# Expert slots: token numbers loaded two slots ahead, results stored by ScalarE's queue, a clamp on VectorE

## The chip, the core and the metric

The kernel runs on one core of a Trainium2 chip. The core has TensorE (PE, with its weight loads shown apart as PEld), VectorE (DVE), ScalarE (ACT), GpSimd (POOL) and SyncE (SP), which issues most of the transfers. The metric is the device time of one execution in microseconds; the time before is the median of three runs, 1485.05 us (1483.12 to 1486.98).

## The reference, cut to what matters

A linear attention makes a matrix x of 4608 tokens by 512. A router gives every token one of eight experts; each expert is a two-layer network with 512 x 1024 and 1024 x 512 weights. A last two-layer network (512 x 2048 x 512) follows.

```python
logits = x @ w_gate + modality_bias[modality_id]
e_idx = np.argmax(logits, axis=1)
gate_w = softmax(logits)[np.arange(N), e_idx]
for e in range(8):
    mask = e_idx == e
    out[mask] = gate_w[mask, None] * (np.maximum(x[mask] @ w1[e], 0.0) @ w2[e])
h = out @ w_in
out = np.maximum(0.01 * h, h) @ w_out
```

## The kernel before

The program has four stages, one after the other: attention and routing (to about 198 us of the span), the experts (to 720 us), the first half of the last network (the class Hidden, to about 1110 us) and its second half. The order of the instructions on every engine is the order in which the code is written; the attention alone is sorted by a table of times.

**Routing.** At its end `phase_r` computes for every token a row number in the DRAM table `region`, in which each expert's tokens lie together, and POOL scatters pairs (token number, gate weight) into it from the tile `tg` (line 384, one indirect DMA for 128 tokens). `tg` has two buffers; ScalarE writes the token numbers into it (line 326). `phase_r` runs five times, the last two for six and three groups of 128 tokens.

**Slots.** The experts' work is cut into slots of 512 tokens of one expert. The table `ti`, computed on the chip, holds for each slot the expert, the place in `region` and the place in the result. SP reads these numbers into registers with `reg` (line 505: a load of one number, then register work) before it issues a transfer with such an address. Ten slots, 0 to 9, are executed here: nine of them unconditional, the others behind a test of their number.

**Inside a slot.** `slot(s)` (line 648) first calls `xload(s + 1)`: SP loads the next slot's 512 pairs from `region` into one of two tiles `idt`, VectorE casts the token numbers to integers (`idi`, line 543), and POOL gathers the rows of x with four indirect DMAs (`xg`, line 545). Then come eight `pass1(f)`, each of 12 matmuls into a bank `hp` of three; ScalarE writes `hh` from it (line 566) and VectorE `hl` (line 567), and a bank is free once its `hl` is written. ScalarE scales `xg` by the gate weights (`xgate`, line 551). Then come four `pass2(s, t)` of 24 matmuls into `yp`; ScalarE copies `yp` into one of two tiles `y` (line 581), and SP stores `y` into the DRAM matrix `dense` (line 582). In the second and third of them TensorE transposes the next slot's `xg` (line 556). Floating numbers are multiplied as a high and a low part; `split` (line 474) makes the high part on ScalarE (line 475) and the low part on VectorE (line 476). Between the passes, `wsplit` splits the weights, which SP loads into a ring of six tiles `st` (line 517).

**The conversions.** The last network's weights come as 64-bit numbers. `f64` (line 597) turns one block of 128 x 1024 such numbers into 32-bit parts, in steps that the slots call: `step()` stands after `pass1(f)` for odd f and after each `pass2`, so two blocks are converted in each of the slots 0 to 7. A block's steps are: the mask on VectorE (610) and the clamp on POOL (611), then two shifts on VectorE (615 and 616; 616 works on the clamped numbers), then two bit operations (618, 619), then four sums (623) and a split into `rh` and `rl`. The first step also has SP store the block before (627, 628) and load the next one (`w`, 594).

SP issues in order. In a slot its queue holds weight loads that wait for a free tile of the ring, the loads and stores of the conversions, the load of `idt`, and the stores of `y`:

```python
nc.sync.dma_start(out=idt.rearrange("p t c -> p (t c)"), in_=region[bass.ds(r, SLOT), :]...)
nc.vector.tensor_copy(out=idi, in_=idt[:, :, 0])
...
nc.scalar.copy(out=y, in_=yp)
nc.sync.dma_start(out=dense[128 * d:128 * d + 128, bass.ds(o, SLOT)], in_=y)
```

Before slot 8 the kernel also has SP load the first tokens of `dense` for the next stage (`xr`, line 755).

Of the kernel before, what the change touches and what calls it, by code (L numbers as in the profile page):

```python
# [9 lines left out]
F32 = mybir.dt.float32  # L10
# [3 lines left out]
AF = mybir.ActivationFunctionType  # L14
ALU = mybir.AluOpType
# [78 lines left out]
def attention(ctx, tc, cst, a, region, xd):  # L94

    nc = tc.nc
    ident, onesf, trib, onesb, biasT, tokid = cst["id"], cst["one"], cst["trib"], cst["oneb"], cst["biasT"], cst["tok"]
    kp = ctx.enter_context(tc.tile_pool(name="kp", bufs=2))
    sp = ctx.enter_context(tc.tile_pool(name="sp", bufs=2))
# [8 lines left out]
    for i in range(4):  # L108
        t = one.tile([128, 4, 146], F32, name=f"kvx{i}")
# [193 lines left out]
    def phase_r(i, c0, c1):  # L303
# [3 lines left out]
        t, rp = {}, {}  # L307

        def r0():
            lr, ri = st_b[i]  # L310
            t["lp"] = sp.tile([128, NC, 8, NE], F32, tag="lp", name="lp", bufs=1)[:, 0:n]
            for x in ("lg", "ex", "w"):
                t[x] = sp.tile([128, NC, NE], F32, tag=x, name=x)[:, 0:n]
            for x in ("mx", "gs"):
                t[x] = sp.tile([128, NC], F32, tag=x, name=x)[:, 0:n]
            for x in ("oh", "st"):
                t[x + "f"] = sp.tile([128, 80], F32, tag=x, name=x)[:, 0:NE * (n + 1)]
                t[x] = t[x + "f"].rearrange("p (e c) -> p e c", e=NE)
            t["tot"] = sp.tile([128, NE], F32, tag="tot", name="tot")
            t["tb"] = sp.tile([128, 2, NE], BF16, tag="tb", name="tb")  # L320
            t["ix"] = sp.tile([128, NC], I32, tag="ix", name="ix")
            t["tg"] = sp.tile([128, NC, 2], F32, tag="tg", name="tg")
            nc.vector.tensor_tensor(out=t["lp"].rearrange("p c (q j) e -> p (c q) j e", q=4),
                                    in0=lr[:, cs].rearrange("p c q (j e) -> p (c q) j e", j=2),
                                    in1=bc(ri[:, cs].rearrange("p c q j -> p (c q) j"), 3, NE), op=ALU.mult)
            nc.scalar.copy(out=t["tg"][:, 0:n, 0], in_=tokid[:, NC * i + c0:NC * i + c1])
# [96 lines left out]
TIMES = {'kmax0': 0.52, 'kmax_t0': 2.07, 'kmax_m0': 2.08, 'kmax_b0': 2.81, 'kexp00': 5.69, 'kexp01': 5.14, 'kmax1': 2.61, 'kmax_t1': 3.96, 'kmax_m1': 3.97, 'kmax_b1': 4.96, 'kexp10': 10.5, 'kexp11': 10.37, 'kv00': -0.98, 'kv01': 1.26, 'kvn00': 1.27, 'kv02': 2.34, 'kv03': 3.62, 'kvn01': 3.63, 'kvT0': 4.15, 'kg0': 5.58, 'kv10': 4.78, 'kv11': 5.01, 'kvn10': 6.83, 'kv12': 7.04, 'kv13': 7.05, 'kvn11': 7.18, 'kvT1': 9.53, 'kg1': 10.5, 'qmax0': 3.34, 'qsub0': 4.01, 'qmax1': 4.06, 'qsub1': 4.45, 'qmax2': 5.72, 'qsub2': 7.63, 'load_k': 7.3, 'load_v': 7.4, 'load_q': 9.28, 'r0': -0.92, 'r1': -0.1, 'r2': 1.0, 'r3': 1.01, 'r4': 1.02, 'r5': 1.03, 'r6': 1.04, 'r7': 1.25, 'r8': 2.6, 'r9': 2.78, 'r10': 3.29, 'r11': 3.3, 'r12': 3.31, 'r13': 3.32, 'r14': 3.33, 'r15': 3.34, 'r16': 3.61, 'scat0': 5.13, 'scat1': 4.64, 'scat2': 7.54, 'scat3': 7.51, 'scat4': 7.24, 'scat5': 8.2, 'scat6': 7.81, 'scat7': 5.6, 'scat8': 9.07, 'trans0': -1.5, 'trans1': -0.08, 'trans2': 0.44, 'trans3': 0.93, 'trans4': 2.62, 'trans5': 2.55, 'trans6': 4.49, 'trans7': 4.66, 'trans8': 6.15, 'xmm0': 0.52, 'xmm1': 0.81, 'xmm2': 1.45, 'xmm3': 3.52, 'xmm4': 4.14, 'xmm5': 5.5, 'xmm6': 6.45, 'xmm7': 7.52, 'xmm8': 10.5, 'evac0': 0.56, 'evac1': 1.32, 'evac2': 3.1, 'evac3': 4.3, 'evac4': 4.91, 'evac5': 5.51, 'evac6': 7.1, 'evac7': 8.89, 'evac8': 10.51, 'prep': -0.05, 'rar0': 5.7, 'rbr0': 0.2, 'rar1': 5.78, 'rbr1': 0.3, 'rar2': 5.86, 'rbr2': 0.4, 'rar3': 5.94, 'rbr3': 0.5, 'rar4': 6.02, 'rbr4': 0.6, 'rar5': 6.1, 'rbr5': 0.7, 'rar6': 6.18, 'rbr6': 0.8, 'rar7': 6.26, 'rbr7': 0.9, 'rar8': 6.34, 'rbr8': 1.0, 'rar9': 6.42, 'rbr9': 1.1, 'rar10': 6.5, 'rbr10': 1.2, 'rar11': 6.58, 'rbr11': 1.3, 'rar12': 6.66, 'rbr12': 1.4, 'rar13': 6.74, 'rbr13': 1.5, 'rar14': 6.82, 'rbr14': 1.6, 'rar15': 6.9, 'rbr15': 1.7, 'rar16': 6.98, 'rbr16': 1.8, 'rascat0': 7.3, 'rascat1': 7.31, 'rascat2': 7.32, 'rascat3': 7.33, 'rascat4': 7.34, 'rascat5': 7.35, 'rbscat0': 2.0, 'rbscat1': 2.01, 'rbscat2': 2.02}  # L423


SP = mybir.EngineType.SP
CLAMP_LO = float(np.array(0x38000000, np.int32).view(np.float32))
CLAMP_HI = float(np.array(0x47EFFFFF, np.int32).view(np.float32))

# [49 lines left out]
def experts(ctx, tc, cst, a, region, xd, dense, did, wops, pre):  # L479
# [14 lines left out]
    hl = wp.tile([128, 8, SLOT], F32R, name="hl")  # L494
    ring = [wp.tile([128, 1024], F32, name=f"st{i}") for i in range(6)]
    NST = len(ring)
    idts = [wp.tile([128, 4, 2], F32, name=f"idt{i}") for i in range(2)]
    idis = [wp.tile([128, 4], I32, name=f"idi{i}") for i in range(2)]
    xg = wp.tile([128, 4, DM], F32, name="xg")
    ys = [wp.tile([128, DM], F32, name=f"y{i}") for i in range(2)]  # L500
# [1 line left out]
    stage, regs = {}, {}  # L502

    def reg(s, f, mx):
        return nc.values_load(ti[0:1, 3 * s + f:3 * s + f + 1], engines=[SP], min_val=0, max_val=mx)

    def wload(s, which, c):
        t = stage[s, which, c] = ring[cnt[0] % NST]
# [14 lines left out]
    def loads_to(n):  # L523
        while nload[0] < min(n, len(items)):
            wload(*items[nload[0]])
            nload[0] += 1

    def wsplit(s, which, c):
# [6 lines left out]
            split(nc, w2h[:, 2 * c:2 * c + 2], w2l[:, 2 * c:2 * c + 2], t.rearrange("p (k f) -> p k f", k=2))  # L535
        loads_to(n + 1 + AHEAD)

    def xload(s):
        r = reg(s, 1, NE * NT)
        idt, idi = idts[s % 2], idis[s % 2]  # L540
        nc.sync.dma_start(out=idt.rearrange("p t c -> p (t c)"),
                          in_=region[bass.ds(r, SLOT), :].rearrange("(p t) c -> p (t c)", t=4))
        nc.vector.tensor_copy(out=idi, in_=idt[:, :, 0])
        for t in range(4):
            nc.gpsimd.indirect_dma_start(out=xg[:, t], out_offset=None, in_=xd,  # L545
                                         in_offset=bass.IndirectOffsetOnAxis(ap=idi[:, t:t + 1], axis=0),
                                         bounds_check=NT - 1, oob_is_err=False)

    def xgate(s):
        for t in range(4):  # L550
            nc.scalar.activation(out=xg[:, t], in_=xg[:, t], func=AF.Copy, scale=idts[s % 2][:, t, 1:2])

    def xprep(k):
        tp = ps2.tile([128, 4, 128], F32, tag="tp", name="tp")
# [15 lines left out]
    def pass2(s, d, o, mid):  # L570
        yp = ps.tile([128, SLOT], F32, tag="y", name="yp")
        n = 0
        for f in range(8):
            for w, h in ((w2h, hh), (w2l, hh), (w2h, hl)):
                nc.tensor.matmul(yp, lhsT=w[:, f, 128 * d:128 * d + 128], rhs=h[:, f], start=(n == 0), stop=(n == 23))  # L575
                n += 1
            if f == 3:
                mid()
        y = ys[cnt[1] % 2]
        cnt[1] += 1  # L580
        nc.scalar.copy(out=y, in_=yp)
# [15 lines left out]
    def f64(cv, name, i, w, ahead, behind):  # L597

        V = nc.vector
        if name == "win":  # L600
            dst = wops["win"][i % 4].rearrange("p s h k f -> h k p s f")[:, i // 4]
        else:
            dst = wops["wout"].rearrange("s p h k f -> h k p s f")[:, i]
        w2 = w.rearrange("p b f w -> p (b f) w")
        lo, hi = w2[:, :, 0], w2[:, :, 1]
        r = cv.tile([128, 8, 256], F32, tag="r", name="r")
        rh = cv.tile([128, 7, 256], F32R, tag="rh", name="rh")
        rl = cv.tile([128, 7, 256], F32R, tag="rl", name="rl")
        t = r[:, 0:4].rearrange("p b f -> p (b f)").bitcast(I32)
        V.tensor_scalar(out=t, in0=hi, scalar1=0x7FFFFFFF, scalar2=None, op0=ALU.bitwise_and)  # L610
        nc.gpsimd.tensor_scalar(out=t.bitcast(F32), in0=t.bitcast(F32), scalar1=CLAMP_LO, scalar2=CLAMP_HI, op0=ALU.max, op1=ALU.min)
        behind()
        ahead()
        yield
        V.tensor_scalar(out=lo, in0=lo, scalar1=29, scalar2=0x40000000, op0=ALU.logical_shift_right, op1=ALU.bitwise_xor)
        V.tensor_scalar(out=t, in0=t, scalar1=4, scalar2=1, op0=ALU.logical_shift_left, op1=ALU.logical_shift_right)
        yield
        V.tensor_tensor(out=t, in0=t, in1=lo, op=ALU.bitwise_xor)
        V.scalar_tensor_tensor(out=t, in0=hi, scalar=-0x80000000, in1=t, op0=ALU.bitwise_and, op1=ALU.bitwise_or)
        yield  # L620
# [27 lines left out]
    def slot(s, step=lambda: None, mid2=lambda t: None):  # L648
# [442 lines left out]
```

## Time and profile before

| | |
|---|---|
| time, median of three runs | 1485.05 us |
| profiled execution: its time, its span | 1477.94 us, 1476.2 us |
| PE busy | 1338.4 us, 91% of the span |
| PEld busy | 1229.8 us, 83% |
| DVE busy | 1031.6 us, 70% |
| ACT busy | 600.5 us, 41% |
| POOL busy | 403.9 us, 27% |
| mean granted clock of TensorE | 0.968 of full speed |

The profile shows one execution. "Busy" is the time in which an engine executes; register work and the issue of transfers are not counted. An idle time stands in brackets before the instruction that ended it, with what released it. A row of SPq is a transfer's issue by SP, not its flight; from issue to landing is told apart. The granted clock is given as a share of 2.4 GHz.

### The profile page before, as it was taken

What the parts mean: (1) busy time and instruction counts of PE and PEld (TensorE: products, weight loads), DVE (VectorE), ACT (ScalarE), POOL (GpSimd) and SP (SyncE); (2) the same over time, 40 slices, a digit from 0 to 9 for tenths busy, and PEclk for the clock granted to TensorE, in tenths of its full rate; (3) what the DMA queues carried; (4) which work ended last, traced back from release to release, by engine and by line L of the source; (5) the groups of instructions that cost most, each with busy time, mean ns of one, the idle gap of its engine ahead of it and who ended that gap; (6) DMA issues with size and microseconds to landing.
All of it is one profiled execution on the core that took longest, in us unless ns stands there. A gap on an engine that the chain in (4) does not pass through costs nothing.

```text
span 1476.2 us, 23214 instructions
## 1 busy us (share of the span) xinstructions
PE 1338.4 (91%) x9083; PEld 1229.8 (83%) x9083; DVE 1031.6 (70%) x1347; ACT 600.5 (41%) x946; POOL 403.9 (27%) x273
## 2 busy tenths in 40 slices
PE   4778718999999999989989999999989999999998
PEld 3668606777777777768889999999989999999998
DVE  5788626677767767634558777777767777777775
ACT  3566414555455545534423223332324333333332
POOL 2447532313231323011033434333331111101111
PEclk9899958999999999989999999999999999999999
DMA  9564245877787779565583333333297443443430
GB/s 374 205 241 154 103 133 171 260 242 233 249 274 232 232 246 305 194 221 179 184 346 144 121 137 136 122 133 125 103 417 295 143 143 117 135 133 118 143 115 30
DMA packets 144519, 280.05 MB, mean 190 GB/s; under 512 B 17808, under 2 KB 69520, under 8 KB 141456
## 3 DMA queue, kind: packets, MB, share of 16 engines
q1 hardware_dynamic: 125376, 218.94, 44.0%
q10 hardware_dynamic: 11472, 38.52, 6.4%
q0 software_dynamic: 7552, 21.02, 4.0%
q8 instruction: 74, 1.21, 0.3%
q14 instruction: 45, 0.37, 0.1%
HBM read 181.59 MB, written 96.85 MB: 189 GB/s over the span
## 4 chain that ended last, share of the span: by engine, by line
issue 26%; DVE 9%; PE 6%; POOL 6%; DMA 2%; ACT 1%; POOLq 0%; SPq 0%; DVEq 0%
PE hp L778 6%; POOL out L959 3%; POOL s L818 2%; DMA wi<-wid 2%; DVE ht L791 1%; DVE ht L824 1%; DVE ht L827 1%; DVE s L815 1%; DVE ht L811 1%; DVE s L813 1%; DVE x L476 1%; POOL s L819 1%; DVE xl L476 0%; ACT ht L820 0%; ACT xh L475 0%
## 5 line engine op out<-in xcount | busy, mean ns | idle before, releaser
L778 PE MATMUL hp<-xh,wi 128*128 128x256 f32 x1152 | 212.9, 281 | 3.7 <-DVE ht L827 2.3
L937 PE MATMUL yp<-wi,x 128*128 128x256 f32 x1152 | 191.5, 284 | 0.0
L778 PEld LDWEIGHTS hp<-xh,wi 128*128 128x128 f32 x1152 | 179.4, 188 | 6.3 <-DVE ht L827 3.8
L937 PE MATMUL yp<-wi,wi 128*128 128x256 f32 x1200 | 178.3, 283 | 0.3 <-DVE wi L476 0.3
L778 PE MATMUL hp<-x,wi 128*128 128x256 f32 x1296 | 166.7, 289 | 8.1 <-DMA wi<-wid 3.9
L778 PEld LDWEIGHTS hp<-x,wi 128*128 128x128 f32 x1296 | 163.1, 197 | 8.9 <-DVE ht L827 4.1
L937 PEld LDWEIGHTS yp<-wi,wi 128*128 128x128 f32 x1200 | 163.5, 192 | 0.5 <-DVE wi L476 0.5
L937 PEld LDWEIGHTS yp<-wi,x 128*128 128x128 f32 x1152 | 161.9, 192 | 0.1
L778 PE MATMUL hp<-xl,wi 128*128 128x256 f32 x576 | 160.8, 279 | 0.0
L564 PE MATMUL hp<-xh,w1h 128*128 128x512 f32 x320 | 129.7, 405 | 27.8 <-DVE hl L567 27.8
L959 POOL DMA_INDIRECT out<-yo,idx x36 | 47.4, 1317 | 314.9 <-DVE idx L953 294.3
L564 PE MATMUL hp<-xl,w1h 128*128 128x512 f32 x320 | 127.6, 399 | 0.0
L564 PE MATMUL hp<-xh,w1l 128*128 128x512 f32 x320 | 127.2, 397 | 0.0
L575 PE MATMUL yp<-hh,w2h 128*128 128x512 f32 x320 | 126.4, 395 | 0.0
L575 PE MATMUL yp<-hl,w2h 128*128 128x512 f32 x320 | 124.8, 390 | 0.0
L575 PE MATMUL yp<-hh,w2l 128*128 128x512 f32 x320 | 124.7, 390 | 0.0
L545 POOL DMA_INDIRECT xg<-xd,idi x44 | 58.3, 1325 | 237.5 <-DVE hl L567 216.8
L818 POOL TENSOR_TENSOR s<-s,s 128x512 f32<-128x512 f32 x36 | 48.3, 1343 | 226.4 <-DVE s L815 160.8
L778 PEld LDWEIGHTS hp<-xl,wi 128*128 128x128 f32 x576 | 108.0, 187 | 0.0
L791 DVE SCALAR_TENSOR_TENSOR ht<-ht 128x1024 f32<-128x1024 f32 x72 | 104.8, 1455 | 2.5
L476 DVE TENSOR_TENSOR w1l<-st,w1h 128x1024 fp32r<-128x1024 f32 x44 | 53.8, 1227 | 71.3 <-ACT w1h L475 71.3
L564 PEld LDWEIGHTS hp<-xh,w1h 128*128 128x128 f32 x320 | 61.9, 193 | 46.9 <-DVE hl L567 34.1
(202 smaller groups left out, 2629.4 us busy)
## 6 DMA issues: line engine op xcount, KB each, us to landing
st<-in_w SPq DMA_DIRECT2D x89, 512.0 KB, 5.1
hd<-ht ACTq DMA_DIRECT2D x72, 512.0 KB, 3.2
xt<-hd SPq DMA_DIRECT2D x18, 1024.0 KB, 5.4
hr<-hd SPq DMA_DIRECT2D x18, 1024.0 KB, 5.5
wi<-wid SPq DMA_DIRECT2D x28, 512.0 KB, 8.4
wi<-wod SPq DMA_DIRECT2D x6, 2048.0 KB, 13.2
v<-in_v SPq DMA_DIRECT2D x8, 1300.0 KB, 13.0
dense<-y SPq DMA_DIRECT2D x40, 256.0 KB, 3.3
```

Of the source, the lines that this page charges most:

```text
L476: nc.vector.tensor_tensor(out=lo, in0=src, in1=hi.bitcast(F32), op=ALU.subtract)
L545: nc.gpsimd.indirect_dma_start(out=xg[:, t], out_offset=None, in_=xd, in_offset=bass.IndirectOffsetOnAxis(ap=idi[:, t:t + 1], axis=0), bou ...
L564: nc.tensor.matmul(hp, lhsT=w[:, k, 128 * f:128 * f + 128], rhs=x[:, k], start=(n == 0), stop=(n == 11))
L575: nc.tensor.matmul(yp, lhsT=w[:, f, 128 * d:128 * d + 128], rhs=h[:, f], start=(n == 0), stop=(n == 23))
L778: self.nc.tensor.matmul(bank[:, g], lhsT=w[:, h, k, 128 * g:128 * g + 128], rhs=x[:, k], start=(n == 0), stop=(n == 5))
L791: V.scalar_tensor_tensor(out=c, in0=c, scalar=0.01, in1=c, op0=ALU.mult, op1=ALU.max)
L811: V.tensor_tensor(out=h[:, 0, 0], in0=bank, in1=s[1], op=ALU.add)
L813: V.tensor_tensor(out=s[6], in0=bank, in1=s[1], op=ALU.add)
L815: V.tensor_tensor(out=s[7], in0=bank, in1=s[6], op=ALU.add)
L818: G.tensor_tensor(out=s[6], in0=s[6], in1=s[5], op=ALU.add)
L937: nc.tensor.matmul(bank, lhsT=x[:, k], rhs=w[i][:, h, k], start=(c == 0), stop=(c == 23))
L959: ins = nc.gpsimd.indirect_dma_start(out=out, out_offset=bass.IndirectOffsetOnAxis(ap=idi[s % 2][:, t:t + 1], axis=0), in_=y[:, t], in_off ...
```

## The change

Five edits, all but the first in the experts' stage.

The tile `tg` gets a third buffer. The load of a slot's pairs becomes a function of its own, `idload`, with three tiles `idt` in place of two. It is called for slots 0 and 1 before the stage's first weights (for slot 0 as the very first transfer, then two weight loads, then slot 1), and in slot s for slot s + 2, behind the copy of slot s's pairs into `did`. The store of `y` is issued by ScalarE, for which `reg` loads the place in the result into a register of ScalarE too. The clamp of the conversions is computed by VectorE, right behind the mask.

```diff
-            t["tg"] = sp.tile([128, NC, 2], F32, tag="tg", name="tg")
+            t["tg"] = sp.tile([128, NC, 2], F32, tag="tg", name="tg", bufs=3)
...
-    idts = [wp.tile([128, 4, 2], F32, name=f"idt{i}") for i in range(2)]
+    idts = [wp.tile([128, 4, 2], F32, name=f"idt{i}") for i in range(3)]
...
-        return nc.values_load(ti[0:1, 3 * s + f:3 * s + f + 1], engines=[SP], min_val=0, max_val=mx)
+        return nc.values_load(ti[0:1, 3 * s + f:3 * s + f + 1], engines=[SP] + [ACT] * (f == 2), min_val=0, max_val=mx)
...
+    def idload(s):
+        if s < NSLOT:
+            nc.sync.dma_start(out=idts[s % 3].rearrange("p t c -> p (t c)"),
+                              in_=region[bass.ds(reg(s, 1, NE * NT), SLOT), :].rearrange("(p t) c -> p (t c)", t=4))
+
     def xload(s):
-        r = reg(s, 1, NE * NT)
-        idt, idi = idts[s % 2], idis[s % 2]
-        nc.sync.dma_start(out=idt.rearrange("p t c -> p (t c)"),
-                          in_=region[bass.ds(r, SLOT), :].rearrange("(p t) c -> p (t c)", t=4))
+        idt, idi = idts[s % 3], idis[s % 2]
         nc.vector.tensor_copy(out=idi, in_=idt[:, :, 0])
...
         nc.scalar.copy(out=y, in_=yp)
-        nc.sync.dma_start(out=dense[128 * d:128 * d + 128, bass.ds(o, SLOT)], in_=y)
+        nc.scalar.dma_start(out=dense[128 * d:128 * d + 128, bass.ds(o, SLOT)], in_=y)
...
         V.tensor_scalar(out=t, in0=hi, scalar1=0x7FFFFFFF, scalar2=None, op0=ALU.bitwise_and)
-        nc.gpsimd.tensor_scalar(out=t.bitcast(F32), in0=t.bitcast(F32), scalar1=CLAMP_LO, scalar2=CLAMP_HI, op0=ALU.max, op1=ALU.min)
+        V.tensor_scalar(out=t.bitcast(F32), in0=t.bitcast(F32), scalar1=CLAMP_LO, scalar2=CLAMP_HI, op0=ALU.max, op1=ALU.min)
...
         nc.sync.dma_start(out=did[bass.ds(o, SLOT)].rearrange("(p t) c -> p (t c)", t=4),
-                          in_=idts[s % 2].rearrange("p t c -> p (t c)"))
+                          in_=idts[s % 3].rearrange("p t c -> p (t c)"))
+        idload(s + 2)
...
+    idload(0)
+    loads_to(2)
+    idload(1)
     loads_to(AHEAD)
     xload(0)
     wsplit(0, 1, 0)
```

SP's queue at the start of the experts' stage before the change; `st_1856` to `st_1861` are the ring's six tiles, `idt_1862` slot 0's pairs, and TENSOR_LOAD reads a number into a register:

```order
L517 DMA st_1856<-in_w 128x4x256
...
L517 DMA st_1860<-in_w 128x2x512
L505 TENSOR_LOAD ti
L505 ISA x2
L541 ISA
L541 DMA idt_1862<-region 128x8
L517 ISA
L517 DMA st_1861<-in_w 128x2x512
```

And the same place after it:

```order
L540 DMA idt_1862<-region 128x8
L505 TENSOR_LOAD ti
L505 ISA x2
L517 ISA
L517 DMA st_1856<-in_w 128x4x256
...
L517 DMA st_1857<-in_w 128x4x256
...
L540 DMA idt_1863<-region 128x8
...
L517 DMA st_1858<-in_w 128x4x256
```

Slot 0's pairs moved from behind five weight loads to the front of them, and slot 1's pairs, which were loaded at the start of slot 0, stand three transfers behind.

ScalarE's queue at the end of slot 0 before the change, from the third `pass2` on; `y_1867` and `y_1868` are the two result tiles, and `rh` and `hh` are as in the text above:

```order
L581 COPY y_1867<-yp 128x512
L475 CAST w1h<-st_1860 128x4x256
L581 COPY y_1868<-yp 128x512
L475 CAST w1h<-st_1861 128x4x256
L475 CAST rh<-r 128x1792
L566 ACTIVATE hh<-hp 128x512
```

And after it:

```order
L583 COPY y_1868<-yp 128x512
L584 ISA
L584 DMA dense<-y_1868 128x512
L475 CAST w1h<-st_1860 128x4x256
L583 COPY y_1869<-yp 128x512
...
L584 DMA dense<-y_1869 128x512
L475 CAST w1h<-st_1861 128x4x256
L475 CAST rh<-r 128x1792
```

Between each copy of a result and the cast of the next weights now stands the store, which has to wait for the copy.

## Rows read from the trace of the kernel before

**Rows 1.** Waits of 185 to 740 us: engine, line, releaser: total us, times, longest

```profile
DVE r L616 <- POOL r L611: 32.6, 9, 4.6
DVE idi L543 <- DMA idt<-region: 32.3, 4, 11.6
ACT y L581 <- DMA dense<-y: 28.5, 6, 5.6
...
PE hp L564 <- DVE hl L567: 27.8, 15, 9.7
...
PE tp L556 <- ACT xg L551: 25.9, 10, 22.6
...
ACT tg L326 <- DMA region<-tg,ix: 7.1, 1, 7.1
```

**Rows 2.** Two slots as stretches: us; busy (instructions) by engine; clock, DMA share, GB/s

```profile
383.40:433.00 49.60, 47.26 (x208) 38.77 (x208) 35.88 (x42) 24.04 (x31) 12.61 (x6) 0.97 0.77 245
...
529.50:577.50 48.00, 46.41 (x209) 37.58 (x209) 34.52 (x42) 24.32 (x31) 12.68 (x6) 1.00 0.78 254
```

**Rows 3.** Timeline of the stage's start: start us, us, engine, line [idle before <-releaser]

```profile
196.41 0.97 POOL L384 DMA_INDIRECT region<-tg,ix  x1 [0.30 <-issue]
196.67 2.92 SPq L517 DMA_DIRECT2D st<-in_w  x5
...
201.82 0.35 SPq L541 DMA_DIRECT2D idt<-region  x1
...
207.28 0.17 DVE L543 CAST idi<-idt 128x4 int32<-128x4 f32 x1 [11.64 <-DMA idt<-region]
...
213.81 0.47 PE L556 MATMUL tp<-cf,xg 128*128 128x128 f32 x1 [22.57 <-ACT xg L551]
```

**Rows 4.** Timeline of slot 0, its first pass

```profile
226.75 1.02 SPq L594 DMA_DIRECT2D w<-in_win  x2
...
236.00 0.17 DVE L543 CAST idi<-idt 128x4 int32<-128x4 f32 x1 [8.65 <-DMA idt<-region]
...
236.83 0.79 PE L564 MATMUL hp<-xh,w1h 128*128 128x512 f32 x1 [5.92 <-DVE hl L567]
...
240.84 0.41 PE L564 MATMUL hp<-xh,w1h 128*128 128x512 f32 x1
```

**Rows 5.** Timeline of slot 8, its first pass

```profile
633.53 0.17 DVE L543 CAST idi<-idt 128x4 int32<-128x4 f32 x1 [8.89 <-DMA idt<-region]
...
634.35 0.79 PE L564 MATMUL hp<-xh,w1h 128*128 128x512 f32 x1 [9.68 <-DVE hl L567]
...
640.06 0.46 PE L564 MATMUL hp<-xl,w1h 128*128 128x512 f32 x1
```

**Rows 6.** Timeline of two slot ends, with the next slots' first waits

```profile
424.32 0.59 ACT L581 COPY y<-yp 128x512 f32<-128x512 f32 x1 [5.59 <-DMA dense<-y]
...
433.09 0.50 PE L564 MATMUL hp<-xh,w1h 128*128 128x512 f32 x1 [2.38 <-DVE hl L567]
...
444.66 0.50 PE L564 MATMUL hp<-xh,w1h 128*128 128x512 f32 x1 [0.38 <-DVE hl L567]
...
520.72 0.59 ACT L581 COPY y<-yp 128x512 f32<-128x512 f32 x1 [3.91 <-PE yp L575]
...
529.50 0.50 PE L564 MATMUL hp<-xh,w1h 128*128 128x512 f32 x1 [0.70 <-DVE hl L567]
```

**Rows 7.** Instructions of lines 616 and 788: ns min/median/max, first and last start

```profile
L616 DVE TENSOR_SCALAR r<-r x16: 671/694/697, 246.9 to 608.7; 128x1024 int32<-128x1024 int32 x16
...
L788 ACTq DMA_DIRECT2D hd<-ht x72: 326/326/335, 737.4 to 1111.3; - x72
```

**Rows 8.** Issue to landing of lines 582 (dense), 541 (idt), 594 (w)

```profile
DMA to landing us min/median/max: 2.0/3.3/10.0
...
DMA to landing us min/median/max: 3.0/3.5/7.4
...
DMA to landing us min/median/max: 7.0/10.1/12.0
```

More of the change, by code (lines that the diff above doesn't have):

```diff
@@ L423 @@
 TIMES = {'kmax0': 0.52, 'kmax_t0': 2.07, 'kmax_m0': 2.08, 'kmax_b0': 2.81, 'kexp00': 5.69, 'kexp01': 5.14, 'kmax1': 2.61, 'kmax_t1': 3.96, 'kmax_m1': 3.97, 'kmax_b1': 4.96, 'kexp10': 10.5, 'kexp11': 10.37, 'kv00': -0.98, 'kv01': 1.26, 'kvn00': 1.27, 'kv02': 2.34, 'kv03': 3.62, 'kvn01': 3.63, 'kvT0': 4.15, 'kg0': 5.58, 'kv10': 4.78, 'kv11': 5.01, 'kvn10': 6.83, 'kv12': 7.04, 'kv13': 7.05, 'kvn11': 7.18, 'kvT1': 9.53, 'kg1': 10.5, 'qmax0': 3.34, 'qsub0': 4.01, 'qmax1': 4.06, 'qsub1': 4.45, 'qmax2': 5.72, 'qsub2': 7.63, 'load_k': 7.3, 'load_v': 7.4, 'load_q': 9.28, 'r0': -0.92, 'r1': -0.1, 'r2': 1.0, 'r3': 1.01, 'r4': 1.02, 'r5': 1.03, 'r6': 1.04, 'r7': 1.25, 'r8': 2.6, 'r9': 2.78, 'r10': 3.29, 'r11': 3.3, 'r12': 3.31, 'r13': 3.32, 'r14': 3.33, 'r15': 3.34, 'r16': 3.61, 'scat0': 5.13, 'scat1': 4.64, 'scat2': 7.54, 'scat3': 7.51, 'scat4': 7.24, 'scat5': 8.2, 'scat6': 7.81, 'scat7': 5.6, 'scat8': 9.07, 'trans0': -1.5, 'trans1': -0.08, 'trans2': 0.44, 'trans3': 0.93, 'trans4': 2.62, 'trans5': 2.55, 'trans6': 4.49, 'trans7': 4.66, 'trans8': 6.15, 'xmm0': 0.52, 'xmm1': 0.81, 'xmm2': 1.45, 'xmm3': 3.52, 'xmm4': 4.14, 'xmm5': 5.5, 'xmm6': 6.45, 'xmm7': 7.52, 'xmm8': 10.5, 'evac0': 0.56, 'evac1': 1.32, 'evac2': 3.1, 'evac3': 4.3, 'evac4': 4.91, 'evac5': 5.51, 'evac6': 7.1, 'evac7': 8.89, 'evac8': 10.51, 'prep': -0.05, 'rar0': 5.7, 'rbr0': 0.2, 'rar1': 5.78, 'rbr1': 0.3, 'rar2': 5.86, 'rbr2': 0.4, 'rar3': 5.94, 'rbr3': 0.5, 'rar4': 6.02, 'rbr4': 0.6, 'rar5': 6.1, 'rbr5': 0.7, 'rar6': 6.18, 'rbr6': 0.8, 'rar7': 6.26, 'rbr7': 0.9, 'rar8': 6.34, 'rbr8': 1.0, 'rar9': 6.42, 'rbr9': 1.1, 'rar10': 6.5, 'rbr10': 1.2, 'rar11': 6.58, 'rbr11': 1.3, 'rar12': 6.66, 'rbr12': 1.4, 'rar13': 6.74, 'rbr13': 1.5, 'rar14': 6.82, 'rbr14': 1.6, 'rar15': 6.9, 'rbr15': 1.7, 'rar16': 6.98, 'rbr16': 1.8, 'rascat0': 7.3, 'rascat1': 7.31, 'rascat2': 7.32, 'rascat3': 7.33, 'rascat4': 7.34, 'rascat5': 7.35, 'rbscat0': 2.0, 'rbscat1': 2.01, 'rbscat2': 2.02}
-SP = mybir.EngineType.SP
+SP, ACT = mybir.EngineType.SP, mybir.EngineType.Activation
 CLAMP_LO = float(np.array(0x38000000, np.int32).view(np.float32))
@@ L550, in xgate @@
         for t in range(4):
-            nc.scalar.activation(out=xg[:, t], in_=xg[:, t], func=AF.Copy, scale=idts[s % 2][:, t, 1:2])
+            nc.scalar.activation(out=xg[:, t], in_=xg[:, t], func=AF.Copy, scale=idts[s % 3][:, t, 1:2])
     def xprep(k):
```

## The prediction, made before the changed kernel was run

> **What bounds the kernel now.** The change lies in the experts' stage, so I read the waits of that stage first. TensorE there waits mostly for VectorE's `hl`, 27.8 us in 15 waits, and for the scaled tokens, 25.9 us, of which 22.57 are one wait before slot 0 [rows 1, 3]. Outside these waits it works without a gap: a slot has 208 or 209 matmuls and transposes in 46.4 us, 0.223 us each, of a period of 48.0 [rows 2]. What a shorter wait saves, the end therefore gains, as long as no other wait takes its place. Next I looked up in the timeline where the waits lie, and what stood in front of the instruction that came late. There are four places: the start, slot 0, slot 8, and the ends of the slots between. The next network's first loads need the memory of the experts, so that stage moves with their end.
>
> **The start.** SP issues slot 0's pairs at 201.82, behind five weight loads from 196.67 on; they are cast at 207.28, and 6.53 us later TensorE starts [rows 3]. In the changed order the pairs are SP's first transfer. They can leave once the last scatter into `region` has landed. POOL issued it until 197.4, and at 201.82 it had landed while the weight loads ran; I take the middle, 199.6. With nothing ahead of them the pairs should need the shortest landing seen, 3.0 us [rows 8], so the cast comes at 202.8, 4.5 us earlier. I leave the 6.53 us as they are, though the weight loads, now some 4 us later, run beside the gathers. The first weights have to be in about 7 us after their issue; if they or the gathers come later, all may be lost. Ends: 0 and 6.9 (pairs out at 197.4). **4.5 us.**
>
> The third buffer of `tg` takes away ScalarE's 7.1 us wait [rows 1], but I cost it at nothing: POOL issues its scatters one behind the other with 0.30 us between them, by issue and not by a wait [rows 3], and the pairs wait for these. Loading slot 1's pairs at the start costs SP an issue of 0.35 us among loads that have time.
>
> **Slot 0.** VectorE's queue stands at the cast of slot 1's pairs for 8.65 us, `hl` is behind it, and TensorE idles 5.92 us [rows 4]. After that, ten matmuls start between 236.83 and 240.84, nine steps of 0.446 us where 0.223 is usual, which is another 2.0 us. With the pairs loaded early the cast waits for nothing. What is late next is the mask of the first conversion, ahead of the third `hl`. Its block `w` is issued at 226.75 in two loads; landings are 7.0 to 12.0 us [rows 4, 8], and I take 8, since less stands ahead of these than of the others. Then `w` is in at 235.3 (0.5 for the second load), mask and clamp end at 236.6 (0.69 each, from line 616 [rows 7]) and `hl` at 237.3. TensorE, going on at 230.9, asks for it two passes of 12 matmuls later, at 236.3. So 1.0 us of wait comes back: 5.92 + 2.0 - 1.0 = **6.9 us**; with `w` after 7.0 or 12.0 us it is 7.9 or 2.9.
>
> **Slot 8.** The same wait, 8.89 us of VectorE and 9.68 of TensorE; the pairs came behind the load of `xr`. Here 13 steps take 5.71 us in place of 2.90, 2.8 more [rows 5]. The pairs will have been loaded in slot 7. What remains is the wait of an ordinary slot's start, 1.03 us by the next part: 9.68 + 2.8 - 1.03 = **11.4 us**, 10.9 to 11.8 by its ends.
>
> **The slots between.** Of the 27.8 us, 12.2 are left in 13 waits: six of 0.35 to 0.40 in the middle of the first pass, 2.2 in all, as at 444.66, and seven at the starts of slots 1 to 7, from 0.70 to 2.38, 10.0 in all [rows 1, 6]. The waits for scaled tokens keep 3.3 us after the first, of which I count half, 1.7, to these slots. One slot shows 0.9 us more of busy time at a granted clock of 0.97 [rows 2]. Together 14.8 us.
>
> At a slot's start, the way from the copy of the last `y` to the first matmul that waits for `hl` is 8.77 us in one slot and 8.78 in another, while the wait is 2.38 and 0.70 [rows 6]. So the wait is 0.70 plus the copy's lateness, and the copy was late because its tile was still being stored (5.59 us of ScalarE's idle time). ScalarE's own store leaves as soon as the copy ends; it then has about 11 us, two passes of 24 matmuls, for a landing of 3.3 us in the median, 10.0 at most [rows 8]. So 0.70 stays. But that store stands between the copy and the cast that begins this way. No row shows ScalarE storing what it has just copied. At best it costs nothing, at worst the copy's 0.59 and an issue of 0.33, 0.92 in all; I take the issue, 0.33 [rows 6, 7]. The first three stores of a slot delay nothing that TensorE waits for, since `yp` has three banks, and the reading of the address into ScalarE's register, once a slot, lies ahead of the first of them. The clamp gives VectorE 16 x 0.69 = 11 us more. In the first pass this replaces a wait of up to 4.6 us for POOL (32.6 in all [rows 1]); in the second pass it lies beside TensorE's work, in a slot in which VectorE is busy for 34.5 of 48.0 us [rows 2]. That cover gone, seven slots would lose 4.8 us. With it, the six middle waits and those for tokens go, since VectorE's sums and with them ScalarE's scaling come earlier. Left are 7 x 1.03 = 7.2 us of 14.8: **7.6 us**, with the ends 3.5 and 9.9.
>
> **Sum.** 4.5 + 6.9 + 11.4 + 7.6 = 30.4 us. The profiled execution took 1477.94 us and would take 1447.5. The median of the runs is 7.1 us above it; from there, 1454.7, say 1455. All lower ends give 17.3 (1467.7), all upper ones 36.5 (1448.6).
>
> **A rule that speaks against the stores.** In the rows the copy waits for `dense<-y` with up to 5.59 us of idle time; they don't tell the issue's delay in SP's queue from the flight. The Trainium skill, page "DMA: Bandwidth & Descriptors", section "Issuing engines are not separate DMA queues", says that transfers of all engines interleave on the same 16 DMA engines, and that issuing from another one saves only the time of its sequencer. No row here shows a store of `y` from ScalarE. What it would make of this kernel is the second rival.
>
> **Rivals.** First, only the two long waits go: the weight loads beside the gathers eat the start, and ScalarE's stores with VectorE's clamps eat the slot ends. For it speaks that both costs are new, and that the landing of `idt` reaches 7.4 us under load [rows 8]; against it, that the clamp replaces a longer wait. 6.9 + 11.4 = 18.3, giving 1467.
>
> Second, the copies stay late, because it is the flight of a store that keeps the tile, and not its place in SP's queue. Then the starts of the slots keep their 10.0 us instead of 4.9: 5.1 less, 25.3, giving 1460. For it: landings of up to 10.0; against it: the median of 3.3 [rows 8].
>
> Third, slower: ScalarE is held at each store for longer than an issue, until the transfer lands or because SP's loads are being issued, and the casts behind it come late at eight slot starts. With x us at each store the gain is 33.1 - 8x: x = 4.1 makes it nothing, and above 4.7 the kernel is slower. At 5.6, the longest wait of ScalarE for a store now [rows 1], it loses 11.7, giving 1497. For it: the store waits for a copy that ends just before. Against it: ScalarE issues 72 stores of `ht` in the next stage at 0.33 us each [rows 7]. At the median landing of 3.3 it would still be 6.7 faster.
>
> That the early loads don't do what they say is hard to see: the pairs of slot s + 2 have a slot of 48 us to land.
>
> **How the numbers follow.** Forecast 70%, first rival 12%, second 11%, third 5%, something else 2%. A difference under 0.3%, 4.5 us, can't be told from none here. Faster has the first three cases, 0.93; the same 0.02; slower 0.05. The range of 80% reaches from the upper ends, with 3 us for the runs' spread, 1446, to the first rival with the same, 1470.
>
> **What would show it.** Right: no idle time of VectorE before `idi` in slots 0 and 8; the first transpose near 209; at slots 1 to 7 waits for `hl` near 1.0 us, all alike, and none in the middle of the first pass; no wait of ScalarE for `dense<-y`. Wrong: first transposes near 213; a wait before the mask of slot 0 of several us; ScalarE standing at line 584 for over a microsecond; starts of slots that wait 2 us and more; or a stage that ends 30 us earlier while the next one starts no earlier.

## The result, and the profile of the changed kernel

The changed kernel took 1451.56 us in the median of four runs (1447.67 to 1452.13) beside 1484.11 us of the kernel before (1483.12 to 1486.98). The ratio is 0.9772, with an interval of 0.9749 to 0.9795, or 30 to 37 us faster. The prediction said 1455 us, 1446 to 1470.

The profiled execution took 1447.67 us. Its span is 1445.5 us. These are the busy times of its page (us, share of the span, instructions):

```profile
PE 1331.2 (92%) x9083; PEld 1228.3 (85%) x9083; DVE 1036.6 (72%) x1363; ACT 604.9 (42%) x946; POOL 342.8 (24%) x257
```

The waits of 185 to 740 us, in the columns of [rows 1]:

```profile
ACT y L583 <- PE yp L577: 58.7, 32, 3.4
...
PE tp L558 <- ACT xg L553: 22.3, 4, 18.3
...
ACT w1h L475 <- ACT y L583: 16.3, 39, 0.5
...
PE hp L566 <- DVE hl L569: 10.8, 9, 1.5
...
DVE r L612 <- DMA w<-in_win: 6.2, 1, 6.2
...
DVE idi L545 <- DMA idt<-region: 5.8, 1, 5.8
```

TensorE waits 9 times for `hl` where there were 15 [rows 1], once in slot 0 and at the starts of eight slots. After the start it has no listed wait for tokens. ScalarE's wait for `dense<-y` and VectorE's for POOL's clamp are not in the view any more, and VectorE waits for `idt` only once, at the start. New are VectorE's 6.2 us for `w` and ScalarE's 0.5 us behind each copy of `y`.

A slot's start, on ScalarE, VectorE and TensorE, to be laid beside [rows 6]:

```profile
413.16 0.59 ACT L583 COPY y<-yp 128x512 f32<-128x512 f32 x1 [3.39 <-PE yp L577]
413.78 0.34 ACTq L584 DMA_DIRECT2D dense<-y  x1
414.16 1.05 ACT L475 CAST w1h<-st 128x1024 fp32r<-128x1024 f32 x1 [0.41 <-ACT y L583]
...
415.24 1.23 DVE L476 TENSOR_TENSOR w1l<-st,w1h 128x1024 fp32r<-128x1024 f32 x1 [1.82 <-ACT w1h L475]
416.38 1.55 DVE L625 TENSOR_TENSOR r<-r 128x256 f32<-128x256 f32 x4
419.70 2.02 DVE L476 TENSOR_TENSOR rl<-r,rh 128x1792 fp32r<-128x1792 f32 x1 [1.76 <-ACT rh L475]
...
421.71 0.69 DVE L569 SCALAR_TENSOR_TENSOR hl<-hp,hh 128x512 fp32r<-128x512 f32 x1
...
420.90 0.39 PE L566 MATMUL hp<-xh,w1l 128*128 128x512 f32 x1
422.45 0.50 PE L566 MATMUL hp<-xh,w1h 128*128 128x512 f32 x1 [1.16 <-DVE hl L569]
422.79 0.40 PE L566 MATMUL hp<-xl,w1h 128*128 128x512 f32 x1
```

The copy follows TensorE at once. The cast behind it begins 1.00 us after the copy's start. In one chain follow the subtraction `w1l`, the conversion's sums, its split and at last the first `hl`. All eight starts wait 1.16 or 1.17 us. A period, with the columns of [rows 2], is now

```profile
375.61:422.45 46.84, 45.68 (x209) 37.62 (x209) 35.40 (x44) 24.51 (x31) 5.12 (x4) 1.00 0.80 259
```

At the start of the stage, beside [rows 3]:

```profile
202.50 0.97 POOL L384 DMA_INDIRECT region<-tg,ix  x1 [0.30 <-issue]
...
206.39 0.17 DVE L545 CAST idi<-idt 128x4 int32<-128x4 f32 x1 [5.78 <-DMA idt<-region]
...
213.51 0.48 PE L558 MATMUL tp<-cf,xg 128*128 128x128 f32 x1 [18.30 <-ACT xg L553]
...
215.50 0.72 ACT L553 ACTIVATE xg<-xg,idt 128x512 f32<-128x512 f32 x1 [2.05 <-DMA xg<-xd,idi]
...
223.43 0.78 PE L566 MATMUL hp<-xh,w1h 128*128 128x512 f32 x1
```

The first pass of the kernel before starts at

```profile
221.29 0.78 PE L564 MATMUL hp<-xh,w1h 128*128 128x512 f32 x1
```

The cast comes 3.89 us behind the last scatter's issue where it came 10.87 behind, so 6.98 us sooner. TensorE's first transpose follows the cast after 7.12 us, before after 6.53; the first pass follows it after 17.04 us, before after 14.01. So 3.03 of the 6.98 us are lost again. ScalarE's scaling of the rows now waits for one gather after the other, up to 2.05 us, and the weight loads, which the old order had ahead of the gathers, run beside them. In slot 0, beside [rows 4]:

```profile
238.43 0.69 DVE L612 TENSOR_SCALAR r<-w 128x1024 int32<-128x1024 int32 x1 [6.21 <-DMA w<-in_win]
...
240.50 0.50 PE L566 MATMUL hp<-xh,w1h 128*128 128x512 f32 x1 [1.49 <-DVE hl L569]
```

**Three stretches.** The routing's last scatter, the first matmul of the first `pass1`, the last copy of `y` and the end of the span cut each profile into parts that can be compared. All numbers are differences of starts in the timelines, in us:

| kernel | last scatter at | to first pass | to last copy | to the end |
|---|---|---|---|---|
| before | 196.41 | 24.88 | 498.72 | 756.2 |
| before, profiled again | 206.97 | 27.27 | 497.68 | 755.4 |
| third `tg` alone | 198.09 | 23.90 | 497.96 | 755.4 |
| store alone | 200.65 | 25.27 | 495.97 | 752.3 |
| clamp alone | 200.27 | 25.32 | 481.86 | 755.6 |
| early pairs alone | 199.08 | 20.78 | 481.78 | 755.4 |
| **changed** | 202.50 | 20.93 | 469.36 | 752.7 |
| changed, profiled again | 206.47 | 21.21 | 469.15 | 752.5 |
| changed, clamp on POOL | 200.17 | 20.93 | 479.14 | 750.5 |
| changed, stores on SP | 197.99 | 21.47 | 469.12 | 755.4 |
| changed, old start | 199.03 | 23.85 | 469.23 | 750.9 |
| changed, later split | 200.68 | 21.06 | 457.41 | 754.2 |
| later split, `w` early | 201.97 | 21.54 | 455.36 | 753.1 |
| later split, stores on SP | 201.86 | 21.57 | 457.21 | 753.4 |

From the first pass to the last copy two executions of one program agree within 1.1 us, so a difference of 2 us or more can be read there. The time of the last scatter differs by 10 us between two executions of the kernel before. From before to changed, the three parts gain 4.0, 29.4 and 3.5 us, 36.8 in all; the changed kernel's profiled execution reached its last scatter 6.1 us later, hence 30.7 us in the spans.

A second reading goes by slots. From slot 1's first matmul to slot 8's, seven slots, it is 340.3 us before (339.0 profiled again), 341.5 with the early pairs alone, 338.4 with the store alone, 324.6 with the clamp alone and 328.0 in the changed kernel. The period of slot 8 is 58.07 us before and 46.83 changed.

### The profile page after: what moved, and what is told of

Same layout as the page of the kernel before. It is cut to its first block, busy times and chain, and to the rows that moved or that the text cites. A ratio compares the mean times of both kernels' runs of the same rounds, so it can differ in the third digit from the quotient of the medians.

```text
span 1445.5 us, 23197 instructions
## 1 busy us (share of the span) xinstructions
PE 1331.2 (92%) x9083; PEld 1228.3 (85%) x9083; DVE 1036.6 (72%) x1363; ACT 604.9 (42%) x946; POOL 342.8 (24%) x257
## 4 chain that ended last, share of the span: by engine, by line
issue 25%; PE 12%; DVE 8%; POOL 6%; ACT 1%; POOLq 0%; DVEq 0%
PE hp L784 12%; POOL out L965 3%; POOL s L824 2%; DVE ht L797 1%; DVE ht L833 1%; DVE x L476 1%; DVE ht L830 1%; DVE s L821 1%; POOL s L825 1%; DVE ht L817 1%; DVE s L819 1%; DVE xl L476 0%; DVE xt L770 0%; DVE xt L772 0%; ACT ht L826 0%
## 5 line engine op out<-in xcount | busy, mean ns | idle before, releaser
L784 PE MATMUL hp<-x,wi 128*128 128x256 f32 x1296 | 163.3, 285 | 8.0 <-DVE ht L797 3.8
L784 PEld LDWEIGHTS hp<-x,wi 128*128 128x128 f32 x1296 | 159.6, 193 | 8.8 <-DVE ht L797 4.0
L547 POOL DMA_INDIRECT xg<-xd,idi x44 | 55.0, 1249 | 398.1 <-DVE hl L569 384.2
L566 PE MATMUL hp<-xh,w1h 128*128 128x512 f32 x320 | 126.5, 395 | 10.8 <-DVE hl L569 10.8
L568 ACT ACTIVATE hh<-hp 128x512 fp32r<-128x512 f32 x80 | 46.9, 597 | 98.2 <-PE hp L566 97.6
```

Of the source, the lines that this page charges most:

```text
L566: nc.tensor.matmul(hp, lhsT=w[:, k, 128 * f:128 * f + 128], rhs=x[:, k], start=(n == 0), stop=(n == 11))
L568: nc.scalar.activation(out=hh[:, f], in_=hp, func=AF.Relu)
L784: self.nc.tensor.matmul(bank[:, g], lhsT=w[:, h, k, 128 * g:128 * g + 128], rhs=x[:, k], start=(n == 0), stop=(n == 5))
```

## The experiments

**One edit at a time, on the kernel before.** The early pairs alone are the diff's edits of `idload`, `xload`, `xgate`, the three `idt` and the start. The other three:

```diff
-        nc.sync.dma_start(out=dense[128 * d:128 * d + 128, bass.ds(o, SLOT)], in_=y)
+        nc.scalar.dma_start(out=dense[128 * d:128 * d + 128, bass.ds(o, SLOT)], in_=y)
...
-        nc.gpsimd.tensor_scalar(out=t.bitcast(F32), in0=t.bitcast(F32), scalar1=CLAMP_LO, ...)
+        V.tensor_scalar(out=t.bitcast(F32), in0=t.bitcast(F32), scalar1=CLAMP_LO, ...)
...
-            t["tg"] = sp.tile([128, NC, 2], F32, tag="tg", name="tg")
+            t["tg"] = sp.tile([128, NC, 2], F32, tag="tg", name="tg", bufs=3)
```

*Early pairs.*

> Only the pairs are loaded two slots ahead (three tiles idt, slot 0's pairs as SP's first transfer); SP stores y, POOL clamps, tg has two buffers. Theory: the start (4), slot 0 (6.9 less a new wait of 1 to 1.5) and slot 8 (11.4, less what late copies keep) are this edit's alone: 21 to 23 us, about 1462. No idle time of VectorE before idi in slots 0 and 8; the waits for hl at slot starts stay unequal (0.7 to 2.4), since the copies of y still wait for their stores. Rival: the late stores of the other slots grow when the pairs no longer hold SP's queue, and the edit alone gives under 18 us.

Measured: 1458.65 us beside 1477.76, ratio 0.9859 (0.984 to 0.9878), 18 to 24 us. VectorE waits for `idt` only at the start, and TensorE's waits for `hl` are

```profile
PE hp L566 <- DVE hl L569: 14.4, 15, 4.6
```

with 4.64 us at the start of slot 1, behind a copy that waited 7.87 us for its tile where an undelayed one is idle for 3.91, so about 4 us late. The theory holds, though the late copies grew in slot 1 as the rival has it: of the 16.9 us in the second column, slot 0 gives 6.5 and slot 8 11.7, and slots 1 to 7 nothing (1.2 longer, within the spread).

*Store.*

> Only the store of y by ScalarE; everything else as before. Theory: the wait of ScalarE for its y tile goes (28.5 us in 6 to 0), seven slot starts change from 10.0 us of wait to 7 x 1.16 = 8.1, so 2 us there; and SP reaches the loads of Hidden some 3.5 us earlier after the last copy, since no store stands ahead of them in its queue. Together 5 to 6 us, about 1479. Rival 1 (flight, not queue, keeps the tile): copies stay late, 0 us. Rival 2 (the hand-over's 3.5 us do not come from SP's freed queue but from elsewhere): 2 us, about 1482, with the first load of Hidden still 7.5 us behind the last copy.

Measured: 1475.05 us, ratio 0.998 (0.9971 to 0.999), 1.5 to 4.3 us. In its waits no copy stands behind a store:

```profile
ACT y L581 <- PE yp L575: 51.2, 24, 3.4
```

The slot starts wait 1.15 or 1.16, and SP's first load for Hidden starts 4.16 us behind the last copy. By the stretches the edit gains 2.8 and 3.9 us. The time shows less than the 5 to 6 us expected; the last scatter came 4.2 us later in the one profiled execution, but whether that holds for the other runs isn't known.

What made a copy late is to be seen at the store of a slot's second result, whose tile the fourth copy needs. In the kernel before, the second copy of one slot ended at 411.41; its store and the time from issue to landing:

```profile
414.50 1.10 SPq L582 DMA_DIRECT2D dense<-y  x1
...
DMA to landing us min/median/max: 9.7/9.7/9.7
```

In slots 0 to 6 this store is issued 2.2 to 3.1 us after the copy's end, behind the conversions' transfers in SP's queue, and lands 8.9 to 10.0 us later where the trace has the landing. The fourth copy would start about 11 us after the second has ended. With the store on ScalarE the second copy of slot 1 ended at 317.90, and its store is

```profile
317.94 0.34 ACTq L582 DMA_DIRECT2D dense<-y  x1
...
DMA to landing us min/median/max: 10.4/10.4/10.4
```

The flight is as long as before, but it begins 0.04 us after the copy, and the fourth copy starts on time at 329.00, 0.7 us after the landing. So it was the delay in SP's queue on top of a long flight that kept the tile, and the flight alone just fits: rival 1 falls, though by a small margin. Rival 2 falls by the last column. The Trainium skill ("DMA: Bandwidth & Descriptors", "Issuing engines are not separate DMA queues") says that another issuing engine saves only the sequencer's time for starting the transfer. In this trace the store was also spared what stood ahead of it in SP's queue, 2.2 to 3.1 us; in the time of the whole kernel little came of it, 1.5 to 4.3 us.

*Clamp.*

> Only the clamp on VectorE. Theory: six waits of 0.35 to 0.40 in the middle of the first pass and some token waits go, 2.2 to 3.9 us, about 1481; waits for hl at slots 0 and 8 stay at 5.9 and 9.7. Rival: 0.69 us of VectorE per block lie on the chain to hl, up to 4.8 us slower, about 1489.

Measured: 1465.03 us, ratio 0.9906 (0.9885 to 0.9928), 11 to 17 us, about three times the theory's upper end; in slots 1 to 7 it gains 15.7 us. VectorE takes for it what the mask takes, and POOL took five times as long. The line in the changed kernel and in the kernel before:

```profile
L613 DVE TENSOR_SCALAR r<-r x16: 693/695/697, 239.2 to 587.8; 128x1024 f32<-128x1024 f32 x16
```

```profile
L611 POOL TENSOR_SCALAR r<-r x16: 3623/3650/4188, 243.2 to 604.6; 128x1024 f32<-128x1024 f32 x16
```

(The Trainium skill, "GPSIMD Engine Reference", section "Engine selection", says of elementwise operations on GpSimd that those with one input run at "roughly line-rate"; for this one the rows differ.) Its waits, with seven slot starts at 0.69 to 1.10:

```profile
PE tp L556 <- ACT xg L551: 24.5, 3, 23.0
...
PE hp L564 <- DVE hl L567: 21.1, 9, 9.6
...
ACT y L581 <- DMA dense<-y: 8.3, 2, 4.3
```

Two copies wait for their tile instead of six. SP's queue also holds the stores and loads of the conversions, and with these faster it moved on: in slots 0 to 6 the second store of a slot is issued 1.0 to 2.1 us after its copy's end, before 2.2 to 3.1. So the store edit has little left to do in the changed kernel. What the rest of the gain is made of, the clamp taken back shows below.

*Third `tg`.*

> Only the third buffer of tg. Theory: ScalarE's 7.1 us wait goes but POOL's scatters leave one behind the other as before, so the last of them and the time stay: 1484, within 0.3%. Rival: the scatters leave earlier by up to the 7.1 us and the experts start earlier, up to 7 us faster; or the end of the routing comes some 6 us later, as the changed kernel's profile had it, which would make the third buffer the cause of that.

Measured: 1477.23 us, ratio 0.9993 (0.9983 to 1.0004). ScalarE's wait of 7.1 us is gone, and the time has not changed, as the theory has it.

**One edit taken back from the changed kernel.** Clamp on POOL:

> The changed kernel with the clamp back on POOL. Theory: a short stop of TensorE costs more than its idle time: from matmul to matmul the middle wait of 0.36 us costs 0.69, and the tokens' wait of 0.28 us costs 0.86 in the stretch of transposes; the clamp removed both in each of six to eight slots, so 1.55 x 7 = 11 us come back (9 to 13): about 2.0 us a slot in the period. Rival: the clamp alone gained 12.7 us because SP's queue went faster by it and the late copies went; with the stores on ScalarE that is no longer there to lose, and only the 2.2 us of idle time in the middle of the first pass plus 1.7 for tokens come back: 3 to 4 us.

Measured: 1454.26 us beside 1480.15, ratio 0.9836 (0.9819 to 0.9853), 9.5 us behind the changed kernel's ratio; 9.8 us in the second column. The period is 48.39 us (seven periods of 278.60 to 617.31) beside 46.85. One slot shows why, TensorE first, then POOL, VectorE and ScalarE:

```profile
386.18 0.39 PE L566 MATMUL hp<-xh,w1l 128*128 128x512 f32 x1
386.94 0.50 PE L566 MATMUL hp<-xh,w1h 128*128 128x512 f32 x1 [0.38 <-DVE hl L569]
387.28 0.40 PE L566 MATMUL hp<-xl,w1h 128*128 128x512 f32 x1
...
397.98 0.83 PE L558 MATMUL tp<-cf,xg 128*128 128x128 f32 x3
399.09 0.77 PE L558 MATMUL tp<-cf,xg 128*128 128x128 f32 x5 [0.28 <-ACT xg L553]
399.61 0.48 PE L577 MATMUL yp<-hh,w2h 128*128 128x512 f32 x1
...
381.91 3.65 POOL L613 TENSOR_SCALAR r<-r 128x1024 f32<-128x1024 f32 x1
...
385.60 0.69 DVE L618 TENSOR_SCALAR r<-r 128x1024 int32<-128x1024 int32 x1 [4.59 <-POOL r L613]
386.20 0.68 DVE L569 SCALAR_TENSOR_TENSOR hl<-hp,hh 128x512 fp32r<-128x512 f32 x1
...
394.89 1.70 ACT L475 CAST rh<-r 128x1792 fp32r<-128x1792 f32 x1 [4.27 <-DVE r L625]
396.49 2.55 ACT L553 ACTIVATE xg<-xg,idt 128x512 f32<-128x512 f32 x4
```

POOL starts the clamp only when the four gathers are issued, here at 381.91. VectorE stands 4.59 us before its shift, with `hl` behind it; ScalarE's cast of the sums and the scaling behind that come late as well. The wait of 0.38 us makes a step of 0.76 and then one of 0.34 where 0.227 is usual, 0.64 us; the wait of 0.28 lengthens the stretch of transposes from 0.79 in the changed kernel, below, to 1.63, so 0.84 us. Together 1.5 us in a slot, the difference of the periods; the theory had 2.0.

```profile
397.51 1.03 PE L558 MATMUL tp<-cf,xg 128*128 128x128 f32 x8
398.30 0.48 PE L577 MATMUL yp<-hh,w2h 128*128 128x512 f32 x1
```

Stores on SP:

> The changed kernel with the stores of y back on SP. Theory: without the late pairs and with the clamp on VectorE, SP's queue moves, the copies are hardly late, and the slot starts wait 0.70 where they wait 1.16 now: 8 x 0.46 = 3.7 us gained; the hand-over to Hidden loses 3.6 (first load 7.7 us behind the last copy): the same time as the changed kernel, within 2 us. Rival: the copies are late as in the kernel before, slot starts 0.7 to 2.4, and the time is 5 to 9 us longer.

Measured: 1446.89 us, ratio 0.979 (0.9771 to 0.9809), not to be told from 0.9772. Seven slot starts wait 0.69 to 0.81, and their periods are 0.45 us shorter, 3.2 in all. But slot 1 waits 2.75 behind a copy that is 2.05 us late (5.96 us of idle time where 3.91 is usual), and the period before it is 3.1 us longer. So the second column shows no gain in place of the 3.7 expected. The hand-over loses what was expected: in its timeline the load of Hidden stands behind the store and a weight load,

```profile
689.19 0.36 SPq L584 DMA_DIRECT2D dense<-y  x1
690.38 0.38 SPq L517 DMA_DIRECT2D st<-in_w  x1
696.12 3.58 SPq L754 DMA_DIRECT2D wi<-wid  x7
```

while in the changed kernel, with the last copy at 692.79, it is

```profile
690.69 0.37 SPq L517 DMA_DIRECT2D st<-in_w  x1
696.87 4.34 SPq L754 DMA_DIRECT2D wi<-wid  x7
```

Those are 7.54 and 4.08 us behind the last copy. SP's store has to wait for the last copy, and the weight load behind it is issued 1.80 us after that copy; without the store it is issued 2.10 us before it. From there to the load of Hidden it is 5.7 and 6.2 us. In the table every kernel with SP's stores has 755.4 to 756.2 in the last column, every one with ScalarE's 750.5 to 752.7, the later split set aside.

Old start:

```diff
-    idload(0)
-    loads_to(2)
-    idload(1)
     loads_to(AHEAD)
+    idload(0)
+    idload(1)
```

> The changed kernel with the start in the old order: five weight loads first, then slot 0's and slot 1's pairs. Theory: the first pass starts 3.9 us later against the last scatter, so 3 to 5 us slower than the changed kernel. Rival: the early pairs gain nothing, because the gathers then run beside the weight loads: 0 to 1 us.

Measured: 1445.70 us, ratio 0.9783 (0.9762 to 0.9803). The time doesn't tell it from the changed kernel, so the 3 to 5 us expected don't show there; the first column has 23.85 in place of 20.93, so 2.9 us. From the cast, at 208.56, to the first pass it is 14.3 us as in the kernel before: so the longer step of the changed kernel goes with its order, in which the gathers run beside the weight loads.

**Later split**, on the changed kernel:

```diff
             pass1(f)
+            if f == 0 and s > 0:
+                wsplit(s, 1, 3)
...
-            if s + 1 < NSLOT:
+            if s + 1 < NSLOT and t < 3:
                 wsplit(s + 1, 1, t)
```

> The changed kernel with one more edit: the last quarter of the next slot's first weights is split behind the next slot's first pass1 and no longer at the end of the slot before. Theory: the wait for hl at eight slot starts (1.16 us of idle time, 1.45 from matmul to matmul) hangs on the cast and the subtraction of that quarter, which stand ahead of the first hh and hl; moved, they leave about 3 us of room, so the eight waits go: period 45.4 us in place of 46.85, 9 to 12 us gained on the changed kernel. Rival: the same work now stands ahead of the second and third hl, and the wait only moves there: 0 to 3 us.

Measured: 1432.75 us beside 1480.15, ratio 0.9687 (0.9673 to 0.9702), 12.6 us below the changed kernel's ratio. No slot start waits; TensorE's waits for `hl` are the one of slot 0 (the row of its wait view), and from 300 to 660 us it was busy throughout, where the changed kernel has 351.86 of 360 us:

```profile
PE hp L566 <- DVE hl L569: 1.7, 1, 1.7
```

```profile
300.00:660.00 360.00, 360.00 (x1652) 299.10 (x1652) 260.57 (x313) 191.90 (x239) 43.47 (x32) 1.00 0.78 259
```

The second column gains 11.95 us for eight waits of 1.16, 1.49 each.

**The kernels once more, and two variants of the later split.**

> The kernel before, profiled once more. In its first profile the last scatter of the routing was issued at 196.41, in the changed kernel's at 202.50, although the instructions up to there are the same but for tg's buffers. Theory: this differs from execution to execution; here it falls anywhere between 196 and 203. Rival: it belongs to the program, and it is again within 0.5 us of 196.4.

Measured: last scatter at 206.97, 10.6 us later than in the first profile of the same program and outside the range of the theory too; one execution of 1489.05 us.

> The changed kernel once more, for its time beside its variants on one chip, and for the last scatter of the routing. Theory: ratio 0.977 within 0.002 as before, last scatter anywhere between 196 and 203. Rival: again within 0.5 us of 202.5, so that the attention of the changed kernel is 6 us slower by its program, which would be taken from the gain in the experts.

Measured: 1450.16 us beside 1484.63, ratio 0.9757 (0.9738 to 0.9776); last scatter at 206.47, again outside the range. On this chip the two programs lie 0.5 us apart, so the 6.1 us between the first two profiles do not belong to the programs, and both rivals fall. Whether the time goes with the execution or with the chip isn't shown: the other two profiles of this round, on the same chip, have 201.97 and 201.86.

`w` early (`next(conv)` stands behind `xload(0)`):

> The version with the later split, and the first conversion's block w loaded before the weights that wait for a free tile of the ring. Theory: slot 0's wait for hl (1.74 us) hangs on the mask, and the mask on w; w is issued some 15 us earlier, the wait goes: 2 us, ratio 0.9675. Rival: the block's transfer delays gathers or weights at the start, and the first pass starts 1 to 4 us later: no gain or slower.

Measured: 1437.16 us, ratio 0.9667 (0.9644 to 0.9689). The wait in slot 0 is gone and the second column 2.05 us shorter, the first 0.5 longer. It is the version with the lowest ratio, 3.3% below the kernel before, though not to be told by time from the later split alone.

Stores on SP:

> The version with the later split, but with the stores of y on SP. Theory: with the later split neither ScalarE's store (0.46 us at a slot's start) nor a copy late by 2 us reaches TensorE, so the slots are alike, and only the hand-over to Hidden is lost, 1 to 4 us (first load 7.5 us behind the last copy in place of 5.5). Rival: no difference, as without the later split, or copies late enough to bring back waits at slot starts.

Measured: 1436.14 us, ratio 0.968 (0.9656 to 0.9705), the same. Here the last column shows no loss (753.4 and 754.2): the later split lengthened it by 1.5 us, with VectorE waiting 6.1 us for ScalarE at the branch into Hidden where the changed kernel has 0.7. Why was not tried.

## Why the prediction was right, point by point

Its sum was 30.4 us; the stretches give 36.8, the median of the runs 32.6. The second measurement of the changed kernel has 34.5 between the medians and 36 by its ratio. The forecast case came true: the waits that it names went, and those left are the ones it says. But the slots between were priced too low by 4.8 us, the 3.5 us of the next stage were not in the sum, and the start came out near its number by luck. Luck too is that the profiled execution took 1447.67 us where the sum gives 1447.5: it is 36.8 us of gain less a routing that ended 6.1 us later.

- **Start**, 4.5 predicted, 4.0 measured, by two errors that cancel. The cast came 6.98 us sooner after the last scatter, not 4.5. "I leave the 6.53 us as they are, though the weight loads, now some 4 us later, run beside the gathers": from the cast to the first pass it is 3.03 us more, with the old order nothing. The sum had this at zero, and the first rival named it. The old-start kernel gives 2.9 of the 4.0; the rest is within the spread of that column (23.85 to 27.27 for the six kernels with the old order). The first transpose came at 213.5 and not near 209, but with a routing that ended 6.1 us later in that execution; behind the last scatter it came after 11.0 us, before after 17.4.
- **Slot 0**, 6.9 predicted, 5.8 measured (65.16 to 58.47 us from the first pass to slot 1's first late matmul, less what slot 1's wait itself changed). The mask is what came late next, as said; it left 1.49 us of wait, not 1.0, and a wait of this kind costs more than it lists: 1.74 us of it were worth 2.05 in the variant with `w` early.
- **Slot 8**, 11.4 predicted, 11.2 measured (142.53 to 129.79 us from 577.48 and 563.00 to the last copy, less 1.5 for the short waits of slot 7).
- **The slots between**, 7.6 predicted, 12.4 measured: the remainder of 29.4. This is the step that was mis-sized. The prediction priced the six middle waits at their idle time, 2.2 us, and the tokens' at 1.7. From matmul to matmul they cost 0.64 and 0.84 us in each of six slots, about 9 together where the sum had 3.9. The mechanism was right: the clamp on VectorE brings sums and scaling earlier.
- **ScalarE's store.** "I take the issue, 0.33": the slot starts went to 1.16 and not 1.03, 0.46 above the 0.70 of an undelayed start. The cast begins 1.00 us behind the copy's start. Before it was 0.48, for the copy at 424.32 [rows 6]:

  ```profile
  424.80 1.05 ACT L475 CAST w1h<-st 128x1024 fp32r<-128x1024 f32 x1
  ```

  The store waits for the copy's end, and the cast for the store's issue. Once the clamp is on VectorE, its price in the second column is as large as what it saves there, one late copy (469.36 with it, 469.12 without). "A landing of 3.3 us in the median" is not what the store had to fit in: the late stores took 9 to 10 us, and 10.4 of about 11 us still fitted.
- **What was not predicted**: the next stage begins 3.5 us sooner after the last copy, since no store of `y` stands ahead of its loads in SP's queue. "The next network's first loads need the memory of the experts, so that stage moves with their end" held, but the distance shrank.
- **The third `tg`**: nothing, as said.

Of the rivals, the first (18.3 us) needed the start and the slot ends to gain nothing, and they gained 4.0 and 12.4; the second (copies late by the flight) fell with the store alone; the third needed x above 4.1 us where 0.46 was measured. The edits alone gain 16.9, 16.9 and 2.8 us in the second column, 36.6 in place of 29.4. Of the 7 us of excess 4 lie in slots 1 to 7: there the clamp alone gains 15.7 us and the changed kernel 12.4. The clamp alone already takes away most of the late copies, and the store on ScalarE then adds its 0.46 us at each slot's start. The early pairs do not thin out the late copies (four waits, 21.7 us, with them alone).

## What to carry to other kernels

Price a short wait by the steps from instruction to instruction around it, not by the idle time that the view lists; eight waits of 1.16 us were worth 12. When several edits relieve the same in-order queue, measure each alone and each taken back; here the sum of the single gains was 7 us too large. When a forecast meets its number, compare the steps too: the start met it by two errors. After a wait has shrunk to the same small value everywhere, look what stands in front of it in program order: here a quarter of the weights that is needed six passes later.

## What the runs showed of the hardware that was not expected

- A stop of TensorE of 0.38 us cost 0.64, one of 0.28 between transposes 0.84, one of 1.16 about 1.49.
- The clamp of 128 x 1024 numbers took 3.65 us on GpSimd and 0.695 on VectorE.
- The second store of a slot, 128 x 512 numbers, took 8.9 to 10.0 us from issue to landing from SP's queue (slots 0 to 6) and up to 10.4 from ScalarE's; the medians of all stores are 3.3 and 4.1.
- Two executions of the same program reached the end of the routing at 196.41 and 206.97 us, while its experts' stage repeated within 1.1 us; whether that goes with the execution or the chip is open.
